# Two attention layers with gated feed-forward: output product and maxima's transpose moved into the filler slots, and more work between the layers

## The chip, the cores and the metric

The kernel runs on one core of a Trainium2 chip. The metric is device time in microseconds (us): the time before is the median of three runs, 2375.84 us (2373.78 to 2376.23). Engines are called as the profile calls them: PE (matrix products; PEld is its weight load), DVE (vector), ACT (activation), POOL, and SP, which here only issues DMAs.

## The reference

Two equal layers run on x (1, 2048, 448). Each is an attention block with 16 query heads of width 28 that share one key head and one value head, and then a gated feed-forward block of width 1792; both have a layer norm in front and a residual behind.

```python
def _A_ref(x, wq, wk, wv, wo):
    q = (x @ wq).reshape(B, S, H, Dh).transpose(0, 2, 1, 3)
    k = x @ wk
    v = x @ wv
    scores = jnp.einsum("bhqd,bkd->bhqk", q, k) * (Dh ** -0.5)
    p = softmax(scores)
    o = jnp.einsum("bhqk,bkd->bhqd", p, v)
    return o.transpose(0, 2, 1, 3).reshape(B, S, H * Dh) @ wo
def _B_ref(x, w_gate, w_up, w_down):
    return (sigmoid(x @ w_gate) * (x @ w_up)) @ w_down
for _ in range(2):
    x = x + _A_ref(_layernorm(x), A_wq, A_wk, A_wv, A_wo)
    x = x + _B_ref(_layernorm(x), B_w_gate, B_w_up, B_w_down)
```

## The kernel before, in words

The order of all instructions is written out by hand in one long Python program; each engine runs its own instructions in that order, and waits only where data or a buffer is missing.

**Tiles.** Queries are cut into U = 16 tiles u of 128 rows, keys into KT = 16 tiles kt of 128. One step of the main loop (L886) is one pair (u, kt), so a layer has 256 steps. Heads are taken in G = 4 groups g of four.

**One step.** ORDER = "FSFSFSFSPXM" (L865) lists what a step issues. Each S is one score product `s` (L488), followed on ACT by the exponential into `P` (L491). P is the value product `pv` of the step before (L499: four 32-column tiles of the array side by side, eight instructions). M is one call of `mx_gen` (L442): four products `mx` (L458; four 32-row tiles of the array side by side, one for each head of a group) against 512 keys, and four maxima `mp` of them on DVE (L462). They find the row maxima that the exponentials of a later query tile need. X advances the side chains (`tick`, L514). Each F is a slice of filler (`Filler.slice`, L743).

**Maxima.** Sixteen calls of M serve one query tile. M runs ahead of the scores: in the main loop the last call for tile u+1 falls in the step kt = 12 of tile u. With the next call, one step later, the code after the loop over key blocks runs: DVE reduces `mp` to `m32` and makes `m16` (L471, L472), and `fin` (L474), queued in `late`, transposes `m16` on PE (`mt`, L477), copies it on DVE (`mr`, L479) and sends it with a DMA from POOL's queue into row 28 of QS, the queries that S reads (L480).

**Side chain of a finished query tile.** `Block.tile` (L535) has stages f0 to ff with a number of ticks before each: f0 and fx bring the sums of the exponentials out, fy inverts them, fz and fw spread them, fa and fb scale the result and split it into two f16 parts `oT`, and `fc` (L584) issues the output product `wo`: 12 matmuls at once (L590). Behind it `f` adds the residual and makes the norm's statistics on DVE, and fd, fe, ff (L599 to L621) make and transpose the normed rows and hand a finished block to the filler. The chain of tile u starts at kt = 1 of tile u+1; fc is reached at kt = 9.

**Filler.** A block is TB = 2 query tiles. Its feed-forward part (`bulk`, L629) makes the gate and up products `gp` and `up` (256 columns wide, through `chain`, L334) and the down product `dn` (L680). Query projections `qp` of 512 rows are also filler (`qgen`, L399; 4 x 11 matmuls). Every matmul has an estimated cost (C512, C448, C256: 216, 190, 110 ns, L84). A slice adds its share of the step's rate to `debt` and issues filler matmuls until the debt is used up; what X issues directly is subtracted from the debt as well (`run`, L738), so that the following slices issue less. The rate (L907 to L911) spreads the work that is left over the steps that are left. Deferred work on ACT and DVE waits in `pend` until `flush`; a lag counts slices (`now`). Stages of `down` (L696 to L722) make the next layer's keys and values of a finished row tile: `db` normalizes, `dc` transposes by DMA, `dd` issues the key and value product `kv` (11 narrow matmuls, L355), `de` transposes the keys by DMA, and `df` counts the tile as done (KVD).

**Banks.** `s`, `mx` and all filler results share seven banks of PSUM (L45).

**Between the layers** (L917 to L930). A loop of ticks with 1800 ns of filler each runs while side chains are open or the 16 calls of M for the next layer's first query tile are not done. A call is made at every fifth tick, and its key block of 512 must be complete (`mx_ready`, L437). The last block's `ff` adds the next layer's query projection 1 to the filler; projections 2 and 3 are added when the layer's main loop starts (L875). Projection 0 was made earlier. `load_qh` (L422) fetches the queries that `mx` reads, and is called when mx_gen starts.

Of the kernel before, what the change touches and what calls it, by code (L numbers as in the profile page):

```python
# [19 lines left out]
def interleaved_layers_kernel(ctx: ExitStack, tc: tile.TileContext, x, wq, wk, wv, wo, wg, wu, wd, out, layers=2):  # L20
# [387 lines left out]
    late = []  # L408
    stored = set()
    LT = 1  # L410
# [26 lines left out]
    def mx_ready(l, n):  # L437

        u, r = divmod(n, 4 * NB)
        return KVD[l] >= 4 * (r // 4 + 1) if u == 0 else True  # L440

    def mx_gen(l):  # L442

        load_qh(l, 0)
        for u in range(U):
            qh = QH[l, u]
            mp = wk1.tile([128, 4, 4, NB], F32, name="mp", bufs=2)
            for kb in range(NB):
                for g in range(G):
                    for i in range(len(late) - 1, -1, -1):  # L450
                        late[i][0] -= 1
                        if late[i][0] <= 0:
                            late.pop(i)[1]()
                    assert KVD[l] >= 4 * (kb + 1)
                    ps = [psf.tile([128, 512], F32, tag=BANKS["m"], name="mx", bufs=NBK[BANKS["m"]])
                          for _ in range(4)]
                    for h in range(4):
                        nc.tensor.matmul(ps[h], qh[32 * h:32 * h + 32, g],  # L458
                                         KK[l][32 * h:32 * h + 32, 1, kb * 512:(kb + 1) * 512], start=True,
                                         stop=True, tile_position=(32 * h, 0))  # L460
                    for h in range(4):
                        nc.vector.tensor_reduce(mp[:, g, h, kb:kb + 1], ps[h], axis=AX.X, op=OP.max)  # L462
                    ps = None
                    if kb == NB - 1 and g == 2 and u + 1 < U:
# [4 lines left out]
            m32 = wk1.tile([128, 16], F32, name="m32")  # L469
            m16 = wk1.tile([128, 16], F16, name="m16")  # L470
            nc.vector.tensor_reduce(m32, mp.rearrange("p g h k -> p (g h) k"), axis=AX.X, op=OP.max)  # L471
            nc.vector.tensor_scalar(m16, m32, -(2.0 ** -15), None, op0=OP.mult)  # L472

            def fin(u=u, m16=m16):  # L474
                stored.add(("m", l, u))
                p = fps([16, 128], F16, "mt")
                nc.tensor.transpose(p, m16, id16)  # L477
                r = wk1.tile([16, 128], F16, name="mr")
                nc.vector.tensor_copy(r, p)  # L479
                nc.gpsimd.dma_start(QS[l, u][28:29].rearrange("o g h n -> o (g h) n"), r)  # L480
            late.append([LT, fin])
        while late:
            late.pop(0)[1]()
# [42 lines left out]
    class Block:  # L526
# [8 lines left out]
        def tile(self, u):  # L535
# [48 lines left out]
            def fc():  # L584
                need(1)
                p = fps([128, D], F32, "wo")
                n = 0
                for h in range(4):
                    for a, c in ((0, 0), (0, 1), (1, 0)):
                        nc.tensor.matmul(p, v["oT"][:, a, h * 128:(h + 1) * 128], WO[:, c, h], start=n == 0, stop=n == 11)  # L590
# [31 lines left out]
            return (1, f0), (1, fx), (1, fy), (1, fz), (1, fw), (1, fa), (1, fb), (2, fc), (2, fd), (3, fe), (2, ff)  # L622
# [47 lines left out]
        def down(self, t, hs):  # L670
# [56 lines left out]
    class Filler:  # L727
        def __init__(self):
            self.gens, self.debt = [], 0.0
# [135 lines left out]
    ORDER = "FSFSFSFSPXM"  # L865
# [4 lines left out]
    for l in range(layers):  # L870
# [4 lines left out]
        if l:  # L875
            for b in range(2, NB):
                fill.add(qgen(l, b), G * QCH)
# [3 lines left out]
        while late:  # L881
            late.pop(0)[1]()
# [3 lines left out]
        for step in range(U * KT):  # L886
            u, kt = divmod(step, KT)
            P = []
            for o in ORDER:
# [8 lines left out]
                elif o == "X":  # L898
                    if u and kt == 1:
# [21 lines left out]
        while (side or pend or fill.gens) if final else (side or pend or done < 4 * NB):  # L921
# [4 lines left out]
            if not final and done < 4 * NB and QDONE.get((l + 1, 0)) == G and mx_ready(l + 1, done):  # L926
                if n >= 5 or done >= 4 * (NB - 1):
# [24 lines left out]
```

## Time and profile before

| what | value |
|---|---|
| device time, median of 3 runs | 2375.84 us (2373.78, 2375.84, 2376.23) |
| profiled execution: span from first to last instruction | 2370.5 us |
| mean granted clock of PE | 0.989 |
| busy PE / DVE / ACT / POOL | 94% / 69% / 66% / 15% |
| layer 0's main loop, about | 117 to 1160 us |
| between the layers, until the next layer's first scores | 1160 to 1284 us |
| layer 1's main loop | 1284 to 2283 us |
| tail | 2283 to 2370.5 us |

The profiled execution's own time is given as its span; the median of the runs is 5.3 us above it. In a row of the trace the columns are: start in us, duration in us, engine, line, operation, the names written and read, the shape, the count of merged instructions, and in brackets the idle time of the engine before it with what ended it. Matmuls are pipelined: the time that one takes from the others is the distance of the starts, not its duration. In the rows of stretches, each engine has its busy time and in brackets a count, and the last three columns are the granted clock, the DMA share and GB/s.

### The profile page before, as it was taken

The page shows a single profiled execution, that of the slowest core. Times are in us where ns is not written, and L with a number is a line of the kernel's source. Part 1 is how long each engine was busy: PE and PEld are TensorE (multiplying, and loading weights), DVE is VectorE, ACT ScalarE, POOL GpSimd, SP SyncE. Part 2 cuts the span into 40 slices and gives each one's busy share as a digit, 9 for nine tenths or more (in the row PEclk, how much of TensorE's full clock was granted, in tenths as well). Part 3 has the DMA queues.
Part 4 walks back from the last instruction along what each step waited for, and adds up shares of the span by engine and source line. Part 5 has one row for each costly group of instructions (what it writes and reads, how often), then busy time and mean ns, then how long its engine had stood idle before and what let it go on. Part 6 is the DMA issues. An engine that isn't in the chain of part 4 may idle for free.

```text
span 2370.5 us, 40937 instructions
## 1 busy us (share of the span) xinstructions
PE 2226.5 (94%) x15592; PEld 990.3 (42%) x15592; DVE 1624.5 (69%) x2858; ACT 1560.6 (66%) x2583; POOL 348.7 (15%) x621
## 2 busy tenths in 40 slices
PE   3688899999999999999999989999999999999999
PEld 1221244444444444444573223444444444444456
DVE  3787787777767777774258887777677776777321
ACT  5497767676667767777513777767676776777751
POOL 5403565001111010101011011000000000000010
PEclk9899999999999999999999999999999999999999
DMA  5433563322223132322342112322232222222133
GB/s 145 132 115 95 155 197 111 102 85 71 90 70 108 55 101 85 91 94 63 108 136 57 27 49 82 95 63 87 62 106 63 89 63 91 86 81 93 57 109 120
DMA packets 227525, 218.57 MB, mean 92 GB/s; under 512 B 159408, under 2 KB 187760, under 8 KB 227328
## 3 DMA queue, kind: packets, MB, share of 16 engines
q1 hardware_dynamic: 220832, 200.11, 28.3%
q0 software_dynamic: 5376, 14.87, 1.7%
q8 instruction: 122, 2.00, 0.3%
q10 hardware_dynamic: 1120, 0.98, 0.1%
q14 instruction: 75, 0.61, 0.1%
HBM read 175.37 MB, written 23.59 MB: 84 GB/s over the span
## 4 chain that ended last, share of the span: by engine, by line
PE 78%; DVE 11%; ACT 3%; DMA 2%; issue 2%; SPq 1%; POOL 0%; ACTq 0%; DVEq 0%; POOLq 0%
PE pv L499 19%; PE s L488 16%; PE dn L680 11%; PE gp L334 10%; PE up L334 10%; DVE mp L462 8%; PE mx L458 6%; PE wo L590 3%; ACT P L491 2%; PE qp L334 2%; DVE st L289 0%; DMA qd<-qst 0%; DMA sums<-rc 0%; DMA lb<-sums 0%; DMA XT<-hl 0%
## 5 line engine op out<-in xcount | busy, mean ns | idle before, releaser
L491 ACT ACTIVATE P<-s,esc 128x512 f32<-128x512 f32 x2048 | 1309.2, 690 | 513.2 <-PE s L488 496.1
L462 DVE TENSOR_REDUCE mp<-mx 128x1 f32<-128x512 f32 x2048 | 1268.2, 683 | 408.0 <-PE mx L458 404.1
L488 PE MATMUL s<-QS,KK 96*128 96x512 f16 x2048 | 761.4, 382 | 61.8 <-DVE mp L462 41.1
L334 PEld LDWEIGHTS <-wgu 128*128 128x128 f16 x4928 | 458.1, 97 | 243.5 <-issue 96.8
L499 PE MATMUL pv<-P,VV 128*32 128x512 f32 x4096 | 549.2, 609 | 0.0
L334 PE MATMUL up<-XT,wgu 128*128 128x256 f16 x2464 | 375.6, 272 | 0.0
L334 PE MATMUL gp<-XT,wgu 128*128 128x256 f16 x2464 | 374.2, 273 | 0.2
L680 PE MATMUL dn<-WD,h 128*128 128x448 f16 x1344 | 321.7, 352 | 0.0
L488 PEld LDWEIGHTS <-KK 96*128 96x128 f16 x2048 | 193.1, 97 | 181.3 <-issue 107.9
L458 PE MATMUL mx<-KK,QH 32*128 32x512 f16 x2048 | 217.8, 389 | 17.3 <-DVE mp L462 5.3
L458 PEld LDWEIGHTS <-QH 32*128 32x128 f16 x2048 | 53.6, 91 | 396.8 <-issue 385.6
L680 PEld LDWEIGHTS <-h 128*128 128x128 f16 x1344 | 124.1, 98 | 135.8 <-issue 22.0
L499 PEld LDWEIGHTS pv<-P,VV 128*32 128x32 f32 x4096 | 81.0, 108 | 206.0 <-issue 193.9
L573 POOL TENSOR_TENSOR lb<-pvs,lb 128x512 f32<-128x512 f32 x32 | 40.5, 1265 | 789.0 <-DMA lb<-sums 647.5
L654 ACT ACTIVATE h<-th 128x512 f16<-128x512 f32 x112 | 70.4, 629 | 86.0 <-DVE th L651 85.8
L295 POOL TENSOR_SCALAR rs<-mv 128x1 f32<-128x1 f32 (+2 forms) x53 | 13.4, 252 | 702.4 <-DVE mv L290 691.6
L651 DVE SCALAR_TENSOR_TENSOR th<-th,up 128x512 f32<-128x512 f32 x112 | 76.1, 679 | 56.9 <-PE up L334 44.4
L334 PE MATMUL qp<-XT,WQ 128*128 128x512 f16 x352 | 108.7, 409 | 2.5 <-DVE mp L462 1.2
L655 DVE SCALAR_TENSOR_TENSOR h<-th,h 128x512 f16<-128x512 f32 x112 | 78.8, 703 | 46.1 <-ACT h L654 46.1
L643 ACT ACTIVATE th<-gp,gsc 128x512 f32<-128x512 f32 x112 | 76.9, 687 | 45.8 <-PE gp L334 45.8
L590 PE MATMUL wo<-WO,oT 128*128 128x448 f16 x384 | 78.3, 353 | 0.2 <-DVE oT L580 0.2
L334 PEld LDWEIGHTS <-WQ 128*128 128x128 f16 x352 | 34.0, 102 | 61.3 <-issue 38.8
(117 smaller groups left out, 787.8 us busy)
## 6 DMA issues: line engine op xcount, KB each, us to landing
wgu<-wgu_d SPq DMA_DIRECT2D x224, 512.0 KB
QS<-qd SPq DMA_DIRECT2D x384, 32.0 KB
lb<-sums SPq DMA_DIRECT2D x128, 64.0 KB
xr<-in_A_x_dram SPq DMA_DIRECT2D x32, 224.0 KB
qd<-qst POOLq DMA_DIRECT2D x28, 256.0 KB, 2.6
wgu_d<-sgu POOLq DMA_DIRECT2D x14, 512.0 KB, 3.8
QH<-qd SPq DMA_DIRECT2D x28, 128.0 KB
x2d<-x SPq DMA_DIRECT2D x16, 224.0 KB
```

The costliest lines, as they stand in the source:

```text
L334: nc.tensor.matmul(ps, a, b, start=n == 0, stop=n == 10)
L458: nc.tensor.matmul(ps[h], qh[32 * h:32 * h + 32, g], KK[l][32 * h:32 * h + 32, 1, kb * 512:(kb + 1) * 512], start=True, stop=True, tile_po ...
L462: nc.vector.tensor_reduce(mp[:, g, h, kb:kb + 1], ps[h], axis=AX.X, op=OP.max)
L488: nc.tensor.matmul(s, KK[l][0:96, 0, kt * 128:(kt + 1) * 128], QS[l, u][:, g].rearrange("p h n -> p (h n)"), start=True, stop=True)
L491: nc.scalar.activation(p, s, AF.Exp, scale=esc)
L499: nc.tensor.matmul(v[32 * g:32 * g + 32], VV[l][:, kt], P[g], start=kt == 0, stop=kt == KT - 1, tile_position=(0, 32 * g))
L590: nc.tensor.matmul(p, v["oT"][:, a, h * 128:(h + 1) * 128], WO[:, c, h], start=n == 0, stop=n == 11)
L643: defer(lambda: nc.scalar.activation(th, gp.rearrange("p j n -> p (j n)"), AF.Tanh, scale=gsc))
L651: nc.vector.scalar_tensor_tensor(t, th, 1.0, up.rearrange("p j n -> p (j n)"), op0=OP.add, op1=OP.mult)
L654: nc.scalar.activation(h[:, 0], t, AF.Copy, scale=2.0 ** -17)
L655: defer(lambda: nc.vector.scalar_tensor_tensor(h[:, 1], t, 2.0 ** -17, h[:, 0], op0=OP.mult, op1=OP.subtract), 1)
L680: nc.tensor.matmul(p, hs[f // 2][:, a, o:o + 128], WD[:, f, c], start=n == 0, stop=n == 3 * FC - 1)
```

## The change

1. `fc` no longer issues the output product. It puts a generator into a new list `fill.urgent`, and every slice issues up to three matmuls of it before the other filler, whatever the debt. When the product is complete, `f` is deferred and fd, fe, ff are started with the same tick counts.
2. ORDER becomes "XFSFSFSFSPM": X stands at the start of a step, between the M of the step before and the first slice, and no longer between P and M.
3. `late` goes. `m32` and `m16` are issued right behind the last four maxima of a query tile, in the same call of M, and the transpose, copy and DMA are deferred by LAG = 4 slices, so that they come at the fourth F of the next step. The DMA goes from SP's queue and no longer from POOL's.
4. For a later layer's first query tile the last key range is cut in two: 512, 512, 512, 256, 256, so 20 calls of M and not 16. A call comes at every third tick, and at every tick for the last four.
5. The last block's `ff` adds query projections 1 and 2, the last row tile's `dd` adds projection 3, and the main loop's start adds none. The queries for the next layer's first maxima are fetched in the last query tile's steps (X, u = 15).

```diff
-    LT = 1
+    LAG = 4
+    KEYS = {False: [0, 512, 1024, 1536, 2048], True: [0, 512, 1024, 1536, 1792, 2048]}
+    def parts_of(l, u):
+        ends = KEYS[l > 0 and u == 0]
+        return list(zip(ends, ends[1:]))
...
+    def row_max(l, u, mp):
+        m32 = wk1.tile([128, 16], F32, name="m32")
+        m16 = wk1.tile([128, 16], F16, name="m16")
+        nc.vector.tensor_reduce(m32, mp.rearrange("p g h k -> p (g h) k"), axis=AX.X, op=OP.max)
+        nc.vector.tensor_scalar(m16, m32, -(2.0 ** -15), None, op0=OP.mult)
+        def fin():
+            stored.add(("m", l, u))
+            p = fps([16, 128], F16, "mt")
+            nc.tensor.transpose(p, m16, id16)
+            r = wk1.tile([16, 128], F16, name="mr")
+            nc.vector.tensor_copy(r, p)
+            nc.sync.dma_start(QS[l, u][28:29].rearrange("o g h n -> o (g h) n"), r)
+        defer(fin, LAG)
...
+                    if k1 == S and g == G - 1:
+                        row_max(l, u, mp)
                     yield
...
-            def fc():
+            def wo_gen():
                 need(1)
...
                 defer(f)
+                later((2, fd), (3, fe), (2, ff))
+            def fc():
+                fill.urgent.append(wo_gen())
+                return
+                yield
...
-                        fill.add(qgen(l + 1, 1), G * QCH)
+                        for n in (1, 2):
+                            fill.add(qgen(l + 1, n), G * QCH)
...
+                if u == NT - 1:
+                    fill.add(qgen(l + 1, 3), G * QCH)
                 yield from kv(l + 1, v["XT"], u % 4, u)
...
             self.debt += ns
+            n = 0
+            while self.urgent and n < 3:
+                c = next(self.urgent[0], None)
+                if c is None:
+                    self.urgent.pop(0)
+                    continue
+                self.debt -= c
+                n += 1
             while self.gens and self.debt > 0:
...
-    ORDER = "FSFSFSFSPXM"
+    ORDER = "XFSFSFSFSPM"
...
-        if l:
-            for b in range(2, NB):
-                fill.add(qgen(l, b), G * QCH)
...
+                    if u == U - 1 and not final and (l + 1, 0) not in QH and QDONE.get((l + 1, 0)) == G:
+                        load_qh(l + 1, 0)
...
-            if not final and done < 4 * NB and QDONE.get((l + 1, 0)) == G and mx_ready(l + 1, done):
-                if n >= 5 or done >= 4 * (NB - 1):
+            if not final and done < last and QDONE.get((l + 1, 0)) == G and mx_ready(l + 1, done):
+                if n >= 3 or done >= last - G:
                     next(mxs[l + 1])
```

More of the change, by code (lines that the diff above doesn't have):

```diff
@@ L437, in mx_ready @@
     def mx_ready(l, n):
-        u, r = divmod(n, 4 * NB)
-        return KVD[l] >= 4 * (r // 4 + 1) if u == 0 else True
+        keys = parts_of(l, 0)
+        return KVD[l] * 128 >= keys[n // G][1] if n < G * len(keys) else True
+    def row_max(l, u, mp):
[11 more added lines that the diff above has]
+        defer(fin, LAG)
     def mx_gen(l):
-        load_qh(l, 0)
+        if (l, 0) not in QH:
+            load_qh(l, 0)
         for u in range(U):
             qh = QH[l, u]
-            mp = wk1.tile([128, 4, 4, NB], F32, name="mp", bufs=2)
-            for kb in range(NB):
+            keys = parts_of(l, u)
+            mp = wk1.tile([128, 4, 4, len(keys)], F32, name=f"mp{len(keys)}", bufs=2)
+            for kb, (k0, k1) in enumerate(keys):
                 for g in range(G):
[L450 to L454, printed above, removed]
+                    assert KVD[l] * 128 >= k1
                     ps = [psf.tile([128, 512], F32, tag=BANKS["m"], name="mx", bufs=NBK[BANKS["m"]])
@@ L457, in mx_gen @@
                     for h in range(4):
-                        nc.tensor.matmul(ps[h], qh[32 * h:32 * h + 32, g],
-                                         KK[l][32 * h:32 * h + 32, 1, kb * 512:(kb + 1) * 512], start=True,
+                        nc.tensor.matmul(ps[h][:, :k1 - k0], qh[32 * h:32 * h + 32, g],
+                                         KK[l][32 * h:32 * h + 32, 1, k0:k1], start=True,
                                          stop=True, tile_position=(32 * h, 0))
                     for h in range(4):
-                        nc.vector.tensor_reduce(mp[:, g, h, kb:kb + 1], ps[h], axis=AX.X, op=OP.max)
+                        nc.vector.tensor_reduce(mp[:, g, h, kb:kb + 1], ps[h][:, :k1 - k0], axis=AX.X, op=OP.max)
                     ps = None
-                    if kb == NB - 1 and g == 2 and u + 1 < U:
+                    if k1 == S and g == 2 and u + 1 < U:
                         load_qh(l, u + 1)
@@ L467, in mx_gen @@
                         load_qs(l, u)
+                    if k1 == S and g == G - 1:
+                        row_max(l, u, mp)
                     yield
[L469 to L483, printed above, removed]
     def scores(l, u, kt, g, P):
@@ L728, in __init__ @@
         def __init__(self):
-            self.gens, self.debt = [], 0.0
+            self.gens, self.urgent, self.debt = [], [], 0.0
         @property
@@ L920, in interleaved_layers_kernel @@
         n = done = 0
-        while (side or pend or fill.gens) if final else (side or pend or done < 4 * NB):
+        last = G * len(parts_of(l + 1, 0))
+        while side or pend or fill.urgent or (fill.gens if final else done < last):
             tick()
```

5 lines of the change are left out of this document (1 added, 4 removed).

## The prediction

> **What bounds the kernel now.** I read the page first, then the table of waits, then the trace step by step.
>
> ```profile
> span 2370.5 us, 40937 instructions
> ...
> PE 78%; DVE 11%; ACT 3%; DMA 2%; issue 2%; SPq 1%; POOL 0%; ACTq 0%; DVEq 0%; POOLq 0%
> ```
>
> The page's chain lies on PE for 78% of the span. Its 11% on DVE is where PE stands behind the maxima. The change takes no product away and adds none, so PE's work stays; only stalls of PE can come or go. All sums below are made against the profiled execution's 2370.5 us; the median of the runs, 2375.84, is 5.3 above it, and I subtract from the median what I subtract from the span. About 0.2%, 4.75 us, is what a measurement of this kernel can tell from no change.
>
> ```profile
> PE s L488 <- DVE mp L462: 41.1, 131, 0.9
> ...
> PE mt L477 <- DVE m L472: 6.9, 12, 1.8
> ```
>
> These are PE's waits for maxima (total, times, longest): the scores wait for a bank that a maximum must free, the transpose waits for `m16`. What the second row says of before is little; what the change makes of it is the main question here.
>
> **Output product (points 1 and 2).** One step in layer 1 in which X issues `wo`, PE alone:
>
> ```profile
> 1940.11 2.44 PE L590 MATMUL wo<-WO,oT 128*128 128x448 f16 x12
> 1942.49 0.39 PE L458 MATMUL mx<-KK,QH 32*128 32x512 f16 x4
> 1942.82 0.39 PE L488 MATMUL s<-QS,KK 96*128 96x512 f16 x1
> 1943.66 0.38 PE L488 MATMUL s<-QS,KK 96*128 96x512 f16 x1 [0.45 <-DVE mp L462]
> 1944.26 0.59 PE L488 MATMUL s<-QS,KK 96*128 96x512 f16 x2 [0.22 <-DVE mp L462]
> 1944.78 1.07 PE L499 MATMUL pv<-P,VV 128*32 128x512 f32 x8
> 1945.78 0.40 PE L458 MATMUL mx<-KK,QH 32*128 32x512 f16 x4
> ```
>
> The product fills 1940.11 to 1942.49, and its debt empties the slices behind it: four scores follow with nothing between them. Two scores take 0.59 where one takes 0.38, so they can follow each other at 0.21; here the second starts 0.84 after the first and the third 0.60 after the second. That is 0.63 + 0.39 = 1.02 us lost, while DVE frees the banks of the four `mx`. With three matmuls of the product in each F, about 0.6 us (2.38 / 4) stands ahead of every score, as filler does in other steps, and the step has no such wait: 1.02 us saved for each product that stands beside an M. M ends in step kt = 12 of u = 14, and fc is at kt = 9, so 14 products of each layer count. The groups confirm it, 168 matmuls in each loop:
>
> ```profile
> 116.00:1098.00 982.00, 34.20 (x168) 9.46 (x14) 0.99 0.33 99
> 1300.00:2222.00 922.00, 34.21 (x168) 9.46 (x14) 1.00 0.24 74
> ```
>
> That is 28 x 1.02 = 28.6 us. The other four products (two in steps without M, two in the ticks behind the loops) gain nothing. Not all of it is kept. The product's estimate, 12 x 190 = 2280 ns, is more than a step's rate, so the next step starts with an empty slice or two, most of all where `gp` and `up` are the filler; the first scores then meet the maxima again, at up to the 0.45 of the row above. I take 0.1 more than before for half of them: -1.4. The DVE work of `f` stays in the step behind the product.
>
> X also holds the narrow `kv` products of layer 0:
>
> ```profile
> 445.01 0.46 PE L334 MATMUL kv<-WKV,XT 128*128 128x56 f16 x11
> ...
> 446.90 0.38 PE L488 MATMUL s<-QS,KK 96*128 96x512 f16 x1 [0.33 <-DVE mp L462]
> ```
>
> ```profile
> 430.00:1095.00 665.00, 4.58 (x110) 1.88 (x10) 4.17 (x20) 1.00 0.28 83
> ```
>
> Its estimate, 11 x 40 ns, also empties a slice, and a score waits 0.33. Behind M, `kv` itself fills that time. Ten of them (110 matmuls) stand beside an M. Between 0.1 and 0.63 each (the larger wait behind `wo`); I take 0.4, near the 0.33 and a little over for DVE work of X that no longer stands between `pv` and the maxima: +4.
>
> Moving X costs nothing on the other queues that I can find: a chain starts one slot earlier, and its sums' DMA waits on SP for the copy of `pv`, with weight loads behind it, but these loads are issued a whole pair of tiles ahead.
>
> **The transpose (point 3).** `m16` is now issued behind the last maximum, but `mt` comes at the fourth F of the next step, a place on PE that it reaches before DVE is done. In one step with `dn` as filler, the last M of a query tile, its maxima and the fourth F:
>
> ```profile
> 1953.79 0.40 PE L458 MATMUL mx<-KK,QH 32*128 32x512 f16 x4
> ...
> 1954.21 2.48 DVE L462 TENSOR_REDUCE mp<-mx 128x1 f32<-128x512 f32 x4 [1.73 <-PE mx L458]
> ...
> 1956.30 0.54 PE L680 MATMUL dn<-WD,h 128*128 128x448 f16 x2
> ```
>
> The same with `gp` and `up` as filler:
>
> ```profile
> 1888.61 0.40 PE L458 MATMUL mx<-KK,QH 32*128 32x512 f16 x4
> ...
> 1890.80 0.60 PE L334 MATMUL up<-XT,wgu 128*128 128x256 f16 x4
> ```
>
> PE comes to the fourth F 2.51 or 2.19 us after M. How early `mt` can run is seen where it waits today:
>
> ```profile
> 113.62 0.22 PE L477 MATMUL mt<-id,m 128*16 128x128 f16 x1 [1.77 <-DVE m L472]
> ...
> 1328.34 0.39 PE L458 MATMUL mx<-KK,QH 32*128 32x512 f16 x4
> ...
> 1331.77 0.22 PE L477 MATMUL mt<-id,m 128*16 128x128 f16 x1 [0.29 <-DVE m L472]
> 1331.92 0.40 PE L458 MATMUL mx<-KK,QH 32*128 32x512 f16 x4
> ```
>
> There nothing stands on DVE between the maxima and `m16`, and `mt` starts 3.43 us after M (0.42 to the first maximum, 2.48 for four, the rest for two small operations and the way to PE). So PE will stand at the fourth F for 3.43 - 2.51 = 0.92 us or 3.43 - 2.19 = 1.24 us. Behind it in PE's order wait the slice's filler, the last score, `pv` and the next M; ACT and DVE run dry. Mean 1.08, for 15 query tiles of each loop: 30 x 1.08 = 32.4 us. The bounds for one are 0.9 and, where DVE has another operation ahead of the maxima, as long as one of them (2.48 / 4 = 0.62), 1.24 + 0.62 = 1.9. `mt` itself takes 0.15 (1331.77 to 1331.92); between `pv` and M part of it hid behind the end of `pv`, so I add 0.1 each, 3. Of the waits that exist, 6.9 - 1.8 = 5.1 us in the loops go. Together -30.3. The 1.77 at the start of layer 0 nearly goes as well, since `m16` is no longer behind the first calls of the new loop: +1.3. SP carries 32 small DMAs more, each waiting for its copy on DVE; the scores need the row three steps later.
>
> **Between the layers (points 4 and 5).**
>
> ```profile
> 1174.57 0.61 PE L458 MATMUL mx<-KK,QH 32*128 32x512 f16 x4 [3.87 <-DMA QH<-qd]
> ...
> 1254.40 3.83 PE L334 MATMUL qp<-XT,WQ 128*128 128x512 f16 x17
> ...
> 1281.65 2.55 PE L334 MATMUL qp<-XT,WQ 128*128 128x512 f16 x11
> 1284.04 1.03 PE L488 MATMUL s<-QS,KK 96*128 96x512 f16 x4
> ```
>
> The wait for the queries (3.87) goes, since they come ahead. From the last down product (1254.40) to the first scores it takes 29.6 us now, for six chunks of `qp` (2.39 each, 1281.65 to 1284.04) and much standing. After the change twelve chunks lie there: 28.7, with two `kv` (0.8), four short M (1.0, under 0.33 each), one M and `mt` (0.5) 31.0 us, 1.4 longer. Seven M more come ahead of that point, 0.33 each or less (1942.49 to 1942.82): 2.1. Net +0.4. If the filler ends ahead of the chain (11 ticks to the last keys and 5 behind, 1.8 us each, 29 us, about the same as the filler), PE would wait for transpose, copy and DMA, which now takes at least the 2.39 from 1281.65 to 1284.04. The bounds are thus -2 and, if all goes smoothly, +1; I take +0.5, since the two lengths are alike. Taking six chunks out of the first 48 steps of layer 1 saves little: one or two `qp` per step lay in waits for maxima there. And with no filler left the debt of two products (2 x 2280 ns) is paid by the first block's steps. I count 0.
>
> **The sum.** +28.6 - 1.4 + 4 - 30.3 + 1.3 + 0.5 = 2.7 us less: 2367.8 for the span, 2373 for the median. What the output product gains, the transpose's new place gives back. With the bounds (product 0.75 to 1.05 each, transpose 0.9 to 1.5, `kv` 0.1 to 0.63, between the layers -2 to +1, and some us for the prepared weights' part of layer 0, which moves with X) this case alone runs from 2360 to 2385.
>
> **Rivals.**
>
> *The transpose doesn't stall.* If PE reached the fourth F later than 3.43 us after M, or went past the waiting `mt`, the 32.4 would not be paid: 2373 - 32 = 2341. Against it stand 2.51 and 2.19, and that today M, one instruction behind `mt`, waits with it (1331.92). The Trainium skill (TensorE: Matmul & The Clock Gate, Part 3, The mechanism) says that PE may pull weight loads ahead but that matmuls start and end strictly in program order; by that rule this rival is shut, and the trace agrees at 1331.77. Chance 0.15, for a place in the order that I misread.
>
> *The product's bank is missed (slower).* `wo` now holds one of seven banks for a step and a half, until `f` behind the next four maxima. A partly made `gp` or `up` holds another one or two, M takes four: a score could wait for a maximum in the very step that should be free, with the 0.45 + 0.22 = 0.67 of the rows above. 28 x 0.67 = 19: 2392. It decides from 0.27 us per product on. Against it: with 0.6 us of product ahead of each score the maxima (0.62 each) keep pace. The Trainium skill (TensorEngine Tiling (Array Packing), Gotcha 1: PSUM Pressure) says that row tiles each need a bank of their own and that this raises the pressure; the waits in the `wo` step agree. Chance 0.13.
>
> *The six chunks are not hidden.* If the stages behind the last tile still stand in line after the filler, or SP's twelve loads of QS, now issued earlier, hold up the transposing DMAs, the stretch grows by 10 and not by 1: 2383. Chance 0.08.
>
> **How the numbers follow.** My case has 0.64: within its spread 0.25 faster by over 0.2%, 0.34 within, 0.05 slower. The first rival adds 0.15 to faster, the second 0.13 to slower, the third 0.07 to slower and 0.01 to same: 0.40, 0.35, 0.25. The range 2352 to 2390 holds my case, the third rival and the milder half of the second; it leaves out most of the first.
>
> **What would show it.** Right: `wo` in groups of three, scores without idle time in those steps, steps of about 4.7 us for 5.7; PE's wait `mt` for `m` grown from 6.9 to 30 us and more in some 30 times of about 1 us; no wait for QH. Wrong: `mt` waits under 10 us (then 2341), or the scores' wait for maxima still near 41 us (then 2390).

## The result and the profile after

| kernel | median | range of the runs | ratio to before, 95% interval | profiled span | granted clock |
|---|---|---|---|---|---|
| before | 2375.72 us | 2373.78 to 2376.23 | 1 | 2370.5 us | 0.989 |
| changed | 2418.43 us | 2414.59 to 2423.79 | 1.0183 [1.0167, 1.0199] | 2417.3 us | 0.978 |

The change makes the kernel 43 us slower; 2373 was forecast, in 2352 to 2390. The page of the changed kernel, span and chain (share by engine):

```profile
span 2417.3 us, 40904 instructions
...
PE 75%; DVE 13%; DMA 3%; ACT 2%; SPq 2%; issue 2%; POOL 2%; ACTq 0%; DVEq 0%; POOLq 0%
```

PE has lost 3 points of the chain, DVE has won 2, DMA, SP and POOL one or two each. PE's waits (total, times, longest):

```profile
PE mt L457 <- DVE m L452: 38.2, 32, 3.0
...
PE s L494 <- DVE mp L481: 23.0, 77, 0.8
PE mx L477 <- ACT P L497: 18.1, 27, 3.8
```

The transpose waits 38.2 us (6.9 before), the scores for maxima 23.0 (41.1 before): both as forecast. The third row is new: M waits 18.1 us for exponentials, for which before has 0.6. No term of the forecast held it.

**The product did what was forecast in its own steps.** PE in one of them, layer 1:

```profile
2112.74 0.40 PE L477 MATMUL mx<-KK,QH 32*128 32x512 f16 x4
2113.07 0.74 PE L596 MATMUL wo<-WO,oT 128*128 128x448 f16 x3
2113.65 0.38 PE L494 MATMUL s<-QS,KK 96*128 96x512 f16 x1
2113.87 0.73 PE L596 MATMUL wo<-WO,oT 128*128 128x448 f16 x3
```

Threes between the scores, nothing in brackets. To see the whole I cut PE's trace into steps, from the first `pv` of a step to the first of the next: 508 in the two loops, and the stretch between them. Sums in us:

| kernel | 30 steps with `wo` | 30 with `mt` | the other 448 | between the layers |
|---|---|---|---|---|
| before | 167.8 | 128.8 | 1738.4 | 128.0 |
| changed | 143.4 | 165.3 | 1771.0 | 130.6 |
| wo_alone (product alone) | 138.5 | 136.6 | 1765.3 | 128.7 |
| x_alone (X alone) | 139.2 | 124.3 | 1741.3 | 128.1 |
| x_wo (both) | 139.5 | 129.4 | 1782.7 | 126.0 |
| mt_alone (transpose alone) | 167.8 | 164.2 | 1746.6 | 133.6 |
| between_alone | 170.0 | 128.5 | 1717.1 | 129.9 |

In the changed kernel the product's steps are 24.4 us shorter and the transpose's 36.5 longer, and the other 448 are 32.6 us longer, although they do the same work or less. Most of what follows is about these 32.6.

**The transpose in the trace.** The changed kernel, the last M of a query tile and `mt`, in a step with filler:

```profile
2196.04 0.40 PE L477 MATMUL mx<-KK,QH 32*128 32x512 f16 x4
...
2196.46 2.48 DVE L481 TENSOR_REDUCE mp<-mx 128x1 f32<-128x512 f32 x4
...
2199.46 0.22 PE L457 MATMUL mt<-id,m 128*16 128x128 f16 x1 [1.06 <-DVE m L452]
```

3.42 us from M to `mt`, 1.06 of it idle. The forecast had 3.43, and waits of 0.92 us with `dn` and 1.24 us with `gp` and `up` as filler; in layer 1 most are 0.75 and 1.06. In a step of layer 1 without filler:

```profile
1415.01 0.40 PE L477 MATMUL mx<-KK,QH 32*128 32x512 f16 x4
...
1415.34 0.82 PE L494 MATMUL s<-QS,KK 96*128 96x512 f16 x3
...
1416.21 2.48 DVE L481 TENSOR_REDUCE mp<-mx 128x1 f32<-128x512 f32 x4
...
1419.20 0.27 PE L457 MATMUL mt<-id,m 128*16 128x128 f16 x1 [3.04 <-DVE m L452]
```

Here the first three slices are empty, PE comes to the fourth F after three scores, and stands for 3.04; DVE also starts the maxima 1.20 us after M and not 0.42, since it has operations of X ahead of them. Three stretches around it show what that does to the clock (length, busy time of PE, PEld, DVE, ACT and POOL, then PEclk):

```profile
1415.80:1419.20 3.40, 0.36 (x2) 0.00 (x0) 3.25 (x8) 1.84 (x3) 1.18 (x2) 1.00 0.00 0
1419.20:1422.60 3.40, 3.40 (x15) 0.63 (x16) 0.36 (x2) 0.69 (x1) 0.00 (x0) 0.51 0.32 62
1422.60:1426.00 3.40, 3.40 (x24) 0.81 (x22) 3.40 (x6) 3.03 (x6) 0.00 (x0) 0.99 0.04 7
```

3.4 us with PE busy for 0.36 are followed by 3.4 us at a granted clock of 0.51. A stretch of 3.4 us at half clock also begins within 1.2 us of the other two waits without filler in this loop, 2.28 us at 1366.9 and 3.05 us at 1473.1. The Trainium skill (TensorE: Matmul & The Clock Gate, Part 1, What's actually happening) says that the array's clock goes to one half after an idle window of about 3.4 us; the trace agrees on the half and on the length, but here the wait was 3.04 us and the window held 0.36 us of work. From the loops' start to the end the changed kernel has 78 us at half clock, before 34.

**ScalarE and SP.** The changed kernel some 20 steps into layer 1's loop:

```profile
1385.68 5.62 SPq L424 DMA_DIRECT2D QS<-qd  x12
...
1391.34 1.82 SPq L574 DMA_DIRECT2D lb<-sums  x4
...
1394.98 1.25 POOL L579 TENSOR_TENSOR lb<-pvs,lb 128x512 f32<-128x512 f32 x1 [68.34 <-DMA lb<-sums]
...
1396.27 0.62 ACT L585 CAST oT<-lb 128x512 f16<-128x512 f32 x1 [3.48 <-POOL lb L579]
1396.79 3.57 ACT L497 ACTIVATE P<-s,esc 128x512 f32<-128x512 f32 x6
...
1397.52 0.37 PE L477 MATMUL mx<-KK,QH 32*128 32x512 f16 x1 [2.11 <-ACT P L497]
```

Read it from below. PE's `mx` waits for a bank that an exponential must free; the exponentials stand on ACT behind the copy `oT` of the side chain; the copy waits 3.48 us for POOL's `lb`, POOL for the four loads of `lb`, and these stand on SP behind the twelve loads of QS (0.47 each). A stop on a side chain has become a stop of PE. In layer 0 another copy does the same:

```profile
456.09 2.48 DVE L481 TENSOR_REDUCE mp<-mx 128x1 f32<-128x512 f32 x4 [0.69 <-PE mx L477]
...
456.44 0.38 PE L494 MATMUL s<-QS,KK 96*128 96x512 f16 x1
...
458.49 0.51 DVE L318 TENSOR_SCALAR xn<-x,mv,rs 128x448 f32<-128x448 f32 x1
...
459.03 0.56 ACT L310 CAST hl<-xn 128x448 f16<-128x448 f32 x1 [3.56 <-DVE xn L318]
459.50 1.26 ACT L497 ACTIVATE P<-s,esc 128x512 f32<-128x512 f32 x2
```

With X at the front `db`'s copy `hl` is queued ahead of the step's exponentials; it waits for `xn`, which stands on DVE behind four maxima. The Trainium skill (the same page, Part 1, Architectural detail) says that ScalarE and VectorE take their instructions strictly in order; the trace agrees: the step's four scores are issued from 456.44 on, while ACT stands for 3.56 us until 459.03.

### The profile page after: what moved, and what is told of

Its sections match the earlier page's. It is cut to its first block, busy times and chain, and to the rows that moved or that the text cites. A ratio compares the mean times of both kernels' runs of the same rounds, so it can differ in the third digit from the quotient of the medians.

```text
span 2417.3 us, 40904 instructions
## 1 busy us (share of the span) xinstructions
PE 2250.9 (93%) x15608; PEld 994.7 (41%) x15608; DVE 1627.5 (67%) x2874; ACT 1573.6 (65%) x2583; POOL 329.0 (14%) x589
## 4 chain that ended last, share of the span: by engine, by line
PE 75%; DVE 13%; DMA 3%; ACT 2%; SPq 2%; issue 2%; POOL 2%; ACTq 0%; DVEq 0%; POOLq 0%
PE pv L505 18%; PE s L494 15%; PE gp L334 10%; PE up L334 10%; DVE mp L481 10%; PE dn L693 9%; PE mx L477 6%; PE wo L596 3%; PE qp L334 2%; ACT P L497 2%; DMA XT<-hl 1%; SPq L424 1%; DMA lb<-sums 1%; SPq L574 0%; DMA wgu<-wgu_d 0%
## 5 line engine op out<-in xcount | busy, mean ns | idle before, releaser
L481 DVE TENSOR_REDUCE mp<-mx 128x1 f32<-128x512 f32 (+1 forms) x2064 | 1270.9, 679 | 468.3 <-PE mx L477 465.6
L505 PE MATMUL pv<-P,VV 128*32 128x512 f32 x4096 | 558.6, 617 | 0.0
L334 PE MATMUL up<-XT,wgu 128*128 128x256 f16 x2464 | 370.6, 273 | 1.8 <-DVE mp L481 1.8
L477 PE MATMUL mx<-KK,QH 32*128 32x512 f16 (+1 forms) x2064 | 232.4, 392 | 28.3 <-ACT P L497 18.1
L693 PEld LDWEIGHTS <-h 128*128 128x128 f16 x1344 | 123.0, 97 | 138.5 <-issue 27.7
L334 PE MATMUL qp<-XT,WQ 128*128 128x512 f16 x352 | 100.4, 415 | 1.8 <-DVE mp L481 1.2
L596 PE MATMUL wo<-WO,oT 128*128 128x448 f16 x384 | 93.6, 355 | 0.4 <-DVE mp L481 0.4
## 6 DMA issues: line engine op xcount, KB each, us to landing
QH<-qd SPq DMA_DIRECT2D x28, 128.0 KB
```

The lines of the kernel that those rows point to most:

```text
L334: nc.tensor.matmul(ps, a, b, start=n == 0, stop=n == 10)
L477: nc.tensor.matmul(ps[h][:, :k1 - k0], qh[32 * h:32 * h + 32, g], KK[l][32 * h:32 * h + 32, 1, k0:k1], start=True, stop=True, tile_positio ...
L481: nc.vector.tensor_reduce(mp[:, g, h, kb:kb + 1], ps[h][:, :k1 - k0], axis=AX.X, op=OP.max)
L505: nc.tensor.matmul(v[32 * g:32 * g + 32], VV[l][:, kt], P[g], start=kt == 0, stop=kt == KT - 1, tile_position=(0, 32 * g))
L693: nc.tensor.matmul(p, hs[f // 2][:, a, o:o + 128], WD[:, f, c], start=n == 0, stop=n == 3 * FC - 1)
```

## Experiments

Ratios are to before, in runs on the same chip; before's median was 2374.4 to 2375.3 us there. A difference between two experiments is taken from their medians; by their ratios it can come out some 2 us otherwise. In the first four, theory A has the transpose and X at the front as two separate losses; the rivals B differ.

**The transpose.**

```diff
-    LAG = 4
+    LAG = 6
```

> The changed kernel with one number changed: the transpose of the maxima is deferred by 6 slices and no longer by 4, so that it comes at the second F of the step after, about 4.9 us behind M where m16 is ready after 3.43. Theory A (two separate losses: the transpose's slice, and X at the front of a step): PE's wait of the transpose for m16 falls from 38.2 us to under 4, and the time from 2418 to 2384 +-5. Rival B (the spread output product itself loses time, and the transpose's wait only stands where PE would wait anyway): the wait falls as well, but waits for maxima or banks grow, and the time falls by less than 12, to 2406 or more.

2375.50 us, 1.0011 [1.0002, 1.0019]: 43 us for two slices (41 by the ratios), nearly all that the changed kernel had lost; better than either theory. With X at its old place:

```diff
-    LAG = 4
-    ORDER = "XFSFSFSFSPM"
+    LAG = 6
+    ORDER = "FSFSFSFSPXM"
```

> Both edits in the changed kernel: transpose deferred by 6 slices, X between P and M. Theory A: the losses add, 2418 - 34 - 20 = 2364 +-7, below the kernel before (2376), since the spread product's gain of about 24 us is left. Rival B: above the kernel before, 2385 or more.

2382.66, 1.0030 [1.0020, 1.0041]: between the two. There `mt` still comes right behind M in some steps (13 waits, 21.0 us in all; lag6_xback):

```profile
552.20 0.39 PE L477 MATMUL mx<-KK,QH 32*128 32x512 f16 x4
552.62 2.48 DVE L481 TENSOR_REDUCE mp<-mx 128x1 f32<-128x512 f32 x4 [1.05 <-PE mx L477]
...
555.62 0.22 PE L457 MATMUL mt<-id,m 128*16 128x128 f16 x1 [3.03 <-DVE m L452]
...
555.78 1.09 PE L693 MATMUL dn<-WD,h 128*128 128x448 f16 x3
```

`down` calls `flush(True)` ahead of its last products, and that runs all deferred work, whatever its lag. l6xb_keep puts the transpose where that does not reach:

```diff
+    rows = []
     def flush(every=False):
+        while rows and rows[0][0] <= now[0]:
+            rows.pop(0)[1]()
...
-        defer(fin, LAG)
+        rows.append((now[0] + LAG, fin))
```

> lag6_xback (the changed kernel with the transpose two slices later and X at its old place, 2382.7) with the deferred transpose on a list of its own, which the forced flushes in down and at the end of a query group do not empty. Theory K (those flushes push the transpose out right behind the maxima, whatever its lag; 21 us of waits for m and 20 us more at half clock): PE's wait for m under 8 us, 2358 (2350 to 2365). Rival M (the waits come from the lag, which two slices more don't cover at that place of X): 2376 or more.

2356.11, 0.9924 [0.9910, 0.9937]: theory K. The wait is gone (l6xb_keep):

```profile
PE mt L461 <- DVE m L456: 4.6, 6, 0.9
```

The steps with `mt` take 131.6 us and not 159.0. Last, the transpose's new place in the kernel before, and nothing else (point 3 of the change):

```diff
-            late.append([LT, fin])
+        defer(fin, 4)
```

> The kernel before with the transpose alone changed: the row maximum right behind its last maxima, transpose four slices later among the filler, its row stored by SP. Theory C: the transpose's own loss is that which lag6 took away, 35 to 45 us, at any place of X and of the product: 2414 (2405 to 2421), PE's wait for m at 35 us and more. Rival D (it costs this only because X at the front and the spread product crowd VectorE): under 2395.

2421.07, 1.0192 [1.0179, 1.0205], that is 45.6 us: theory C, at its upper end. The waits (mt_alone):

```profile
PE mt L450 <- DVE m L445: 39.4, 32, 4.1
```

So 32.5 us of it are waits (39.4 - 6.9). Its time at half clock is 61 us against 34, which is 13.5 us at most if PE had full work there; together 46.

**X and the product.**

> The changed kernel with the order of a step set back, X between P and M again; the product stays spread, the transpose stays at its fourth slice. Theory A: X at the front puts ACT's and DVE's operations of X ahead of the step's exponentials (the trace shows ACT waiting 3.56 us for xn behind four maxima, with four scores standing) and the spreading of the sums behind twelve loads on SP; with X back these waits go, ACT's wait of hl for xn from 69 to about 33 us and that of oT for lb from 34 to about 6, and the time falls to 2398 +-6. Rival B: the place of X is neutral, 2412 to 2424.

X back alone (ORDER "FSFSFSFSPXM", LAG = 4): 2417.87, 1.0186 [1.0172, 1.0199], no change from 2418.43. I took X for neutral; it is a gain and a loss of one size. Cut into steps, X at its old place makes the 448 others 24 us and the product's steps 5 us shorter, and the transpose's steps 26 us longer (its wait is 53.7 us, for 38.2). Before with the spread product alone (point 1 of the change, its core here):

```diff
-            return (1, f0), (1, fx), (1, fy), (1, fz), (1, fw), (1, fa), (1, fb), (2, fc), (2, fd), (3, fe), (2, ff)
+            return (1, f0), (1, fx), (1, fy), (1, fz), (1, fw), (1, fa), (1, fb), (2, fc)
...
+            while self.urgent and n < 3:
```

> The kernel before with the spread output product alone (the list of urgent matmuls, three in each slice; order of a step, transpose, key ranges and projections as before). Theory A: the steps with the product shrink from 5.66 to 4.6 us (28 of them, -29), the steps behind them lose some 0.2 to 0.4 (-6): 2376 - 23 = 2353 +-6. Rival B: 2376 or more, with scores waiting for banks in and behind these steps.

2378.26, 1.0014 [1.0005, 1.0023]: 3.3 us slower, in rival B's range, but not for its reason, since the scores' wait for maxima falls (29.0 us, 41.1 in before). The table says where: 29.3 us less in its steps, 34.7 more in all the others, 7.8 of them in the transpose's steps. Before with X alone:

```diff
-    ORDER = "FSFSFSFSPXM"
+    ORDER = "XFSFSFSFSPM"
```

> The kernel before with X alone moved to the front of the step; product whole, transpose and the stretch between the layers as before, load_qs as before. Theory E (X at the front puts lb's loads right behind QS on SP, which cost 30 us in lag6, and ScalarE's hl copy ahead of the exponentials, 10 us): 2405 (2395 to 2415), ScalarE's oT waits for lb at 30 us and more. Rival L (both cost that only beside the spread product, whose twelve matmuls want oT): 2380 or less.

2341.36, 0.9863 [0.9850, 0.9877]: 32.5 us faster. Theory E is refuted, and rival L's bound is far passed. PE in x_alone, a step with `wo`:

```profile
2040.97 0.39 PE L458 MATMUL mx<-KK,QH 32*128 32x512 f16 x4
2041.30 2.44 PE L590 MATMUL wo<-WO,oT 128*128 128x448 f16 x12
2043.58 1.03 PE L488 MATMUL s<-QS,KK 96*128 96x512 f16 x4
2044.54 0.64 PE L499 MATMUL pv<-P,VV 128*32 128x512 f32 x4
```

The whole product stands behind M and not ahead of it, so the four maxima (2.48 us on DVE) run beside it, and the four scores follow without a wait. This step takes 4.57 us, the spread one 4.58. X takes by itself the 28.6 us that I gave to the spread, and the other 448 steps grow by no more than 2.9 us. Both:

> The kernel before with X at the front and the output product spread, nothing else of the change (transpose late, stretch between the layers and load_qs as before). X alone gave 2341.4, the spread product alone 2378.3. Theory P (X at the front takes by itself what the spread product was to gain, since a whole product behind M covers M's maxima; the spread then adds only its costs, a step without filler for each new block, weights loaded a step later on SP and lb's loads later still): 2362 (2352 to 2376), more than ten of ScalarE's oT waits for lb. Rival Q (the two gains are one and the spread costs nothing beside it): 2338 to 2346.

2381.16, 1.0028 [1.0017, 1.0040]: 40 us slower than X alone; theory P, past the end of its range. The product's steps are the same (139.5 us for 139.2), the 448 others 41.4 us longer. ScalarE's copy `oT` (count, busy and mean ns, idle before it), in x_alone:

```profile
L579 ACT CAST oT<-lb 128x512 f16<-128x512 f32 x32 | 19.7, 615 | 13.0 <-POOL lb L573 13.0
```

and in x_wo:

```profile
L579 ACT CAST oT<-lb 128x512 f16<-128x512 f32 x32 | 19.7, 617 | 33.3 <-POOL lb L573 33.3
```

SP's rows show why the spread makes `lb` later. In x_alone, query tile 5, whose steps 2 and 5 begin at 435.62 and 447.23:

```profile
436.07 5.60 SPq L419 DMA_DIRECT2D QS<-qd  x12
...
444.71 1.96 SPq L568 DMA_DIRECT2D lb<-sums  x4
```

In x_wo the same steps begin at 452.65 and 464.48:

```profile
452.54 2.40 SPq L633 DMA_DIRECT2D wgu<-wgu_d  x2
...
454.99 7.33 SPq L419 DMA_DIRECT2D QS<-qd  x12
...
465.35 1.72 SPq L568 DMA_DIRECT2D lb<-sums  x4
```

By the code a new block's filler starts a step later with the spread product, and its weight loads now stand on SP for 2.40 us right ahead of QS, whose own twelve take 7.33 us and not 5.60. `lb`'s loads come 0.9 us after the start of step 5 and not 2.5 us ahead of it.

**SP's queue and ScalarE's copy.** Two edits, first together on lag6:

```diff
-                    if kb * 4 + g == 7:
+                    if kb * 4 + g == 10:
...
-                v["hl"] = ln_split(v["x2"], *v["ls"], eng=nc.vector, hi=nc.scalar.copy)
+                v["hl"] = ln_split(v["x2"], *v["ls"], eng=nc.vector, hi=nc.vector.tensor_copy)
```

> The changed kernel with the transpose two slices later (as in lag6, 2375.5), the fp16 copy of the second layer norm's split (in db) on VectorE in place of ScalarE, and load_qs issued three M later (at 10 for 7), so that the twelve loads of QS no longer stand on SP's queue ahead of the loads of lb. Theory C (X at the front puts ScalarE's copy, which waits for VectorE, ahead of the step's exponentials, and SP's lb loads behind QS): the excess of the kv steps and the steps behind them falls from 18 to 6 us, ScalarE's waits for lb and xn go, M's wait for the exponentials halves; 2363 (2359 to 2367). Rival D: the waits move to VectorE, which now does the copy as well: 2372 or more.

2335.18, 0.9834 [0.9821, 0.9847]: 40 us, more than theory C had. The first alone (QS loads three M later):

> lag6 with load_qs alone issued three M later. Theory E: oT's waits for lb go (34 us in all on ScalarE), the kv steps stay as they are; 2359 (2353 to 2365). Rival F: 2371 or more, with oT's waits gone and nothing gained.

2345.36, 0.9875 [0.9862, 0.9889]: 30 us for twelve loads moved by three steps, 8 us past theory E's range. `oT` in lag6_qs:

```profile
L585 ACT CAST oT<-lb 128x512 f16<-128x512 f32 x32 | 19.7, 617 | 6.3 <-POOL lb L579 6.2
```

In lag6 that wait was 34.1, and M's for exponentials falls with it, from 18.0 us to 2.2, although ACT's `hl` still waits 68.8 us for `xn`. So the stop that reached PE's M was `oT`'s. The copy alone:

> lag6 with the copy alone moved from ScalarE to VectorE, load_qs where the change has it. Theory E (the 40 us that lag6_hlqs lost against lag6 are two waits on ScalarE, which X at the front puts ahead of the step's exponentials: hl for xn, 16 times in layer 0, and oT for lb, 32 times in both layers): the kv steps' 15 us and a part of the unfilled steps' go, 2352 (2346 to 2358), the oT waits stay at 34 us. Rival F (the copy alone does it, lb's loads are hidden): 2340 or less.

2382.43, 1.0035 [1.0022, 1.0049]: 7 us slower than lag6, neither theory. So the copy's 10 us (lag6_qs to lag6_hlqs) are there only once SP's queue is free; 7 of them lie in the ten `kv` steps beside an M and those behind them (87.0 to 79.9 us). lag6_hl's loss lies in the same steps, 101.3 us for 95.4 in lag6: each tile's first pair is shorter, its second longer. Why is open; the trace has 58 us at half clock, lag6's 41. In the kernel before both together:

> The kernel before with the same two edits (copy on VectorE, load_qs three M later). Theory E: there X stands at the end of a step, ScalarE waits little for xn or lb, so there is little to gain: 2371 (2366 to 2376). Rival G (the two edits speed up any such kernel, and have nothing to do with the change): 2345 or less.

2370.63, 0.9981 [0.9972, 0.9990]: theory E; all but some 5 us of what they remove is made by the change. And on the changed kernel with its LAG of 4:

> The changed kernel with the transpose where the change puts it (four slices later), with both edits. Theory E: the transpose's own loss is as large as between lag6 and after, so 2335 + 43 = 2378 (2370 to 2384), which would be what the blind sum gave for a spread product that keeps its gain and a transpose that gives it back. Rival H (with ScalarE's waits gone the maxima come earlier and the transpose waits less): under 2362.

2369.82, 0.9977 [0.9968, 0.9986]: just below theory E's range; beside the edits the transpose's place costs 35 us (lag6_hlqs to after_hlqs) and not 43. With these two waits gone the change comes out 5 us ahead of before, where the forecast had 2.7; ahead of before with the same two edits it is 0.8 us, which is within the noise. The spread product alone with QS moved:

> The kernel before with the output product spread alone (as in wo_alone, 2378.3), and load_qs three M later (at 10 for 7). Theory E (SP's twelve QS loads ahead of the loads of lb hold up oT, here in 8 tiles for 14 us, and the stops bring half-clock stretches, 54 us against 34): 2366 (2360 to 2371). Rival J (with X at the end of a step the spread product gains nothing, whatever SP does): 2376 or more.

2370.09, 0.9982 [0.9973, 0.9991]: theory E, 8 us back of the 35.

**The empty step.** The spread ends each block's turn one step later, and the rate still drains the filler for the old step, so a step without filler stands ahead of each new block. `FIRST` is the step for which the rate aims:

```diff
-    FIRST = KT * TB + 16
+    FIRST = KT * TB + 17
```

> The changed kernel with the transpose two slices later (as in lag6, 2375.5) and FIRST raised from +16 to +17, so that the filler of each pair of tiles is spread over one step more. Theory C (what the spread product saves, some 25 us, is given back in places that can be named; one is a step without filler ahead of each new block, since a block's bulk now comes one step later while the rate still drains the filler for the old step): 14 such steps are filled again, some 8 us less, 2367 (2364 to 2370), and fewer steps under 3.2 us. Rival D (the steps have a floor set by ScalarE and VectorE, so that filler moved from one step to another saves nothing): 2373 or more.

2379.20, 1.0021 [1.0011, 1.0030], and on wo_alone:

> The kernel before with the output product spread alone (as in wo_alone, 2378.3; X, transpose and the stretch between the layers as before) and FIRST raised from +16 to +17. Theory C: the empty step goes here too, 2368 (2365 to 2371). Rival D: 2375 or more.

2374.66, 0.9997 [0.9987, 1.0006]. Theory C wanted 8 and 10 us; it got 4 us lost (2 by the ratios) and 4 won, and the intervals of each pair overlap. In lag6_first the steps with maxima and fewer than six filler matmuls, those of product and transpose left out, fall from 97 to 87, as meant. Its trace also has `mt` waiting 6.5 us (2.0 in lag6), but that is one execution of 2386.2 us, the slowest of lag6_first, beside lag6's fastest. The empty step is there; that filling it gains what theory C wanted is not shown.

**Between the layers.** Before with points 4 and 5 of the change alone:

> The kernel before with the part between the layers alone (four query chunks groups ahead of layer 1, key ranges 1536 to 1792 to 2048, M every third tick, first QH loaded early); the transpose where it was, product and X as before. The blind sum had +0.5 us here and 0 for layer 1's first steps: 2374 (2371 to 2377). The other reading of the trace, by which layer 1's steps without query chunks became 9 us shorter and the stretch 2.6 us longer: 2368 (2364 to 2370).

2358.62, 0.9931 [0.9918, 0.9943]: 16.4 us, neither reading reached it. Layer 1's first 48 steps and the `qp` in them (stretch, its length, busy time of PE with the count, DVE, ACT), in before:

```profile
1287.72:1450.54 162.82, 24.52 (x64) 4.23 (x7) 3.64 (x6) 0.99 0.14 40
```

and in between_alone:

```profile
1294.50:1434.61 140.11, 0.00 (x0) 0.00 (x0) 0.00 (x0) 0.98 0.10 27
```

The 48 steps are 22.7 us shorter for 64 `qp` matmuls less, which back to back are 13.9 us (2.39 / 11 each), and the stretch between the layers that took most of them is only 1.9 us longer. One step of each shows why. In before, a step that has no filler matmul either:

```profile
1387.88 0.39 PE L458 MATMUL mx<-KK,QH 32*128 32x512 f16 x4
...
1388.20 0.60 PE L488 MATMUL s<-QS,KK 96*128 96x512 f16 x2
...
1389.05 0.38 PE L488 MATMUL s<-QS,KK 96*128 96x512 f16 x1 [0.23 <-DVE mp L462]
...
1389.64 0.38 PE L488 MATMUL s<-QS,KK 96*128 96x512 f16 x1 [0.22 <-DVE mp L462]
```

In between_alone:

```profile
1329.43 0.39 PE L479 MATMUL mx<-KK,QH 32*128 32x512 f16 x4
1329.76 1.22 PE L499 MATMUL s<-QS,KK 96*128 96x512 f16 x4
1330.90 1.06 PE L510 MATMUL pv<-P,VV 128*32 128x512 f32 x8
```

Four scores in a row take 1.14 us, and the step 2.47, as long as DVE's four maxima (2.48). In before the third and fourth score wait for a maximum, and the step takes 3.07. So do most steps there with one `qp` and many with two: the matmul itself is not what costs 0.6 us. What the slow steps share is an open product. In before a `qp` product has two of its eleven matmuls at 1366.75 and 1367.78 and the third at 1394.34, and by the code it holds one of the seven banks from its first matmul to its copy. I counted the steps without filler (with one M; product, transpose and the step behind a product left out) in before and between_alone: in 35 such a product is open, and none of them takes under 2.79 us; in 40 none is open, and 27 of these take 2.47 to 2.55. That the held bank is the reason is read from the code and the waits; no run changes the number of banks.

**Together.** x_between is before with X at the front, the part between the layers, and the two edits of lag6_hlqs; product whole, transpose late.

> The kernel before with X at the front and the part between the layers, and with the copy on VectorE and load_qs three M later; product whole, transpose late as before. Theory N (what the parts gave alone adds, once SP's queue is out of the way: 33.5 and 16.3 us, and some 5 us of the kv steps for the copy): 2320 (2313 to 2327). Rival O (layer 1's first steps without filler become too short for ScalarE and VectorE, and the parts overlap): 2331 or more.

2302.08, 0.9697 [0.9684, 0.9711]: 72 us faster than before, 116 faster than the changed kernel, and past theory N's range. PE's waits for maxima and `m` (x_between):

```profile
PE s L499 <- DVE mp L483: 19.8, 49, 1.5
...
PE mt L457 <- DVE m L452: 5.8, 6, 1.8
```

M waits 0.2 us for exponentials, 8.8 in x_alone, and the time at half clock is 14 us, 34 in before. Compared with lag6_hlqs the product's steps are the same (136.5 and 137.2 us), the transpose's 9.0 us shorter, and the other 448 are 20.8 us shorter. Counted in the trace, as time above the filler's own, lag6_hlqs has twelve steps more with fewer than six filler matmuls, and the steps behind a product with maxima cost it 7 to 8 us more; with some 12 us or more for the steps with little filler that is most of the 20.8 us. This is a count of where the time lies; no run takes these steps away alone.

## Why the prediction was wrong

The sum failed where it added the spread product (+27.2) to X at the front (+4) with the sentence "Moving X costs nothing on the other queues that I can find". For X alone the sentence holds, and X gains 32.5 us; beside the spread product it fails, and the two together give -6.6 us (x_wo) where the sum had 31.2. I had looked at weight loads and sums on SP, not at the twelve QS loads that the changed kernel has right ahead of `lb`'s, and not at what X puts on ACT ahead of the exponentials. The runs put 30 us (lag6 to lag6_qs) and 10 us (lag6_qs to lag6_hlqs) there, and the two edits together 49 us on the changed kernel itself. With both out of the way it takes 2369.8, and I had said 2373.

That this agrees is partly luck, since the terms were wrong in both directions (us gained):

| step | forecast | alone | by |
|---|---|---|---|
| product spread | +27.2 | -3.3 | wo_alone |
| X at the front | +4 | +32.5 | x_alone |
| transpose at the fourth F | -30.3 | -45.6 | mt_alone |
| between the layers and layer 1's first steps | +0.5 and 0 | +16.4 | between_alone |
| sum | 2.7, with +1.3 for layer 0's start | 0.0 | |

The parts alone sum to nothing, the change is 43.5 slower, and the difference is mostly X beside the spread: x_wo is 1.0028, where 0.9863 and 1.0014 would make 0.9877; 0.0151 of 2375 is 36 us.

- *Product.* Right for its steps (28.6 forecast; 24.4 in the changed kernel, 29.3 alone). Wrong that this is the spread's: X gives the same 28.6. Wrong that hardly any of it (1.4) is given back: alone 34.7 are. Of these 8 are SP's queue (wo_qs). Counted above the filler's own time, 8 lie in the transpose's steps, 8 in the steps behind a product, and the rest is about the twelve steps more with little filler; the one run aimed at those, FIRST, gave no clear gain. The rival by which the product's bank is missed is not what happened in the product's own steps: the scores' wait for maxima fell to 23 us.
- *X.* The +4 was priced from `kv` alone, and `kv` gains nothing: its ten steps and those behind them take 84.7 us in x_alone, 82.8 in before, 96.9 in the changed kernel. I had in front of me the row of `wo` ahead of M with 1.02 us lost behind it, and did not ask what moving all of `wo` behind M does.
- *Transpose.* Mechanism right, and the step with filler nearly (0.92 and 1.24 forecast, 0.75 and 1.06 measured). Mis-sized by 15 us, since I priced no step without filler (five waits of 2.3 to 3.0 us) and no clock (13.5 us at most in mt_alone). The rival that it doesn't stall is refuted.
- *Between the layers.* The wait for QH went, as forecast, and the stretch is 2 to 3 us longer; the failed step is "I count 0" for layer 1's first steps, because I took a `qp` beside a wait for maxima for free. While such a product is open, many steps take 3.07 us and not 2.47.
- *Start of layer 0.* +1.3 forecast; the loop starts at 121.2 us after 119.8, so nothing came.

Open are: why the second `kv` steps of a tile grow in lag6_hl, what makes the spread's last 20 us beyond the count of where they lie, and what FIRST's step costs in lag6_first.

## What to carry to other kernels

Where a side chain shares in-order queues with the main loop, a step moved by half a slot is priced by what its instructions then stand ahead of and behind on every queue; follow PE's new wait back to the first queue that was late, here twelve loads on SP. Before splitting a block of work to cover a wait, see whether moving it whole behind the instruction that starts the wait covers it too. Price a product that trickles through the loop by what it holds while it is open, not by its matmuls alone. Measure the parts of a change alone as well as together: a part worth 32 us and one worth 16 lay hidden in a change that lost 43.

## What the runs showed of the hardware

- A wait of PE of 3.04 us was followed by 3.4 us at a granted clock of 0.51, so PE paid for that stall behind its end as well.
- Four scores in a row take 1.14 us up to the next `pv`, and their step 2.47; in before and between_alone no step without filler takes under 2.79 us while a `qp` product is open, and many take 3.07.
- Twelve DMA issues on SP take 5.6 us (0.47 each), more than two steps of 2.47 us: an issue behind them is late by its queue alone.
